# Two quarters of h gated in PSUM and copied out by ScalarE, and a longer queue before VectorE takes unhurried sums

## The chip, the cores and the metric

The program runs on one NeuronCore of a Trainium2 chip. The metric is the device time of one execution in microseconds, as the median of several runs. TensorE (PE) multiplies matrices into PSUM, eight banks of 512 fp32 columns. VectorE (DVE) and ScalarE (ACT) read and write PSUM and SBUF, GpSimd (POOL) works on SBUF alone, and SyncE (SP) issues the DMAs.

## The reference

Linear attention on 4 x 576 tokens feeds a mixture of eight experts, whose gate is normalised in eight Sinkhorn rounds, and then one wide feed-forward layer. What matters for the change is the expert layer and the last layer:

```python
for e in range(E):                      # E = 8; x is 2304 x 512, w1[e] 512 x 1024
    h = np.maximum(x @ w1[e], 0.0)
    out += P[:, e:e+1] * (h @ w2[e])    # w2[e] 1024 x 512
...
h = x @ w_in                            # 512 x 2048
g = h * (1.0 / (1.0 + np.exp(-1.702 * h)))
return g @ w_out                        # 2048 x 512
```

## The kernel before

Every matrix is split in two fp32r halves (a high part and the rest), and a product is three matmuls. Each 2 x 2 block product is done in seven products instead of eight, by sums of quarters of x, h and the weights. A *pair* is 512 columns of one expert's F (two halves c = 0 and 1 of 256 columns); a *visit* is one pair on one of three columns of 768 tokens. There are 16 pairs and 48 visits in layer 0 (the experts, `l` = 0) and 4 pairs and 12 visits in layer 1 (the last layer).

A visit makes h in `up_fast` (L1183), once for each half c, and multiplies it by w2 in `down_across` (L1346) in layer 0, `down` in layer 1. In `up_fast` the function `prod` multiplies one quarter of the weights into a bank (six matmuls on PE). The quarters of h are A11 (bank 2, called `pc`, the same bank for both halves), A22 (bank 7, `q`, the same for both), A12 (`ri`, bank 1 or 4) and a fourth that is never stored (`le`, bank 0 or 3). From them come S2, S1, N3 and S4, sums of quarters (`mixed`, L1221). `operand` (L1251) splits one of these seven into its high part `h..0` (an ACT copy) and the rest `h..1` (a subtraction). The subtraction is a DVE instruction if the source is a PSUM bank, and otherwise an SBUF sum of kind `VP`, which DVE or POOL may take. The tile names in rows and orders read h, half c, number of the operand (0 A11, 1 A12, 2 S2, 3 S1, 4 N3, 5 S4, 6 A22), part: `h161` is the rest of A22 of half 1. `gate` (L1233) applies ReLU and the token's gate P, of which a broadcast lies in `x2s`; layer 0 gates h itself from expert 1 on, and expert 0 is gated later in `acc`.

In layer 0 from expert 1 on, A11 and A22 are gated by DVE from their bank into the `ring` (SBUF buffers of 128 x 384), and their high part and rest are then made from the ring. A12 and the fourth quarter are gated in their banks. In layer 1, A11 and A22 stay in their banks, `operand` copies them to h and (argument `kept`) to the ring with two ACT copies, and DVE subtracts from the bank.

`down_across` goes through 14 turns of six matmuls (`TURNS`, L1329): A11 of both halves, S1 of half 0, A12 of both, S2 of both, S1 of half 1, then N3, S4 and A22 of both. After A11, ACT copies banks 5 and 6 into banks 0 and 1 (L1369), on which A12 goes on adding; S1 starts in banks 7 and 2; and from S2 on each group's end is added to `acc` by DVE (L1375) before the group's banks are used again.

The order of each engine's instructions comes from a planner (`Plan`, L27 on): it walks a list of all operations with their costs and due times and hands each engine the most urgent one that is ready. `VP` operations wait in one heap for DVE and POOL. DVE leaves the most urgent of them to POOL when its due time is more than `BELOW` = 2.5 us away and fewer than six are waiting (L152). PE's own order is fixed by the code. Beside all this, DVE and POOL turn the last layer's weights from fp64 words into fp32 (`double_piece`, L1113: six DVE operations of 128 x 512 on `x2s` at L1125 to L1141 and one POOL sum, 32 times, with due times from 440 to 1400 us), and POOL subtracts the high parts of all weights (`split`, L1094: `w1x` and `w2x`). Between the layers `y_operands` (L1024) makes layer 1's x from `acc` by more `VP` sums.

Of the kernel before, what the change touches and what calls it, by code (L numbers as in the profile page):

```python
# [24 lines left out]
class Plan:  # L25
# [86 lines left out]
    def run(self):  # L112
# [10 lines left out]
        m, done, t, bus, drift, out = 0, 0, 0.0, 0.0, 0.0, []  # L123
        self.stall = []
        while done < len(self.ops):
# [8 lines left out]
            for e in ("X", "PE", "DVE", "POOL", "ACT", "SP"):  # L134
# [12 lines left out]
                elif e in ("DVE", "POOL"):  # L147
                    own, both = sets[e], sets["VP"]
                    flex = both[0][2] if both else None
                    if flex is not None:  # L150
                        slack = flex.late - t + drift
                        if e == "DVE" and slack > self.BELOW and len(both) < 6:  # L152
                            flex = None
                        if e == "POOL" and slack < flex.dur["POOL"] - flex.dur["DVE"] and at["DVE"] < t + 0.5:
                            flex = None
# [45 lines left out]
def tile_performer_sinkhorn_moe(  # L201
# [981 lines left out]
    def up_fast(l, e, j, c):  # L1183
# [23 lines left out]
        def ring_of(i):  # L1207
            return (lambda: RT(i)), ("ring", i)

        def bank_of(b):  # L1210
            return (lambda: o(b)), ("b", b)
# [21 lines left out]
        def gate(b, th, out=None):  # L1233
            out = out or bank_of(b)
            rec(
                "DVE", ps_us(Q),
                lambda e: e.scalar_tensor_tensor(  # L1237
                    out=out[0](), in0=o(b), scalar=0.0, in1=T["G"][th], op0=ALU.max, op1=ALU.mult
                ),
                [("b", b), ("G", th)], [out[1]],  # L1240
            )
# [37 lines left out]
        for slot in (3, 2) if c == 0 else (2, 3):  # L1279
            yield  # L1280
            if slot == 3:
                prod(le, 3, 2, False)
                act(lambda: RT(u2), lambda: o(le), [("b", le)], [("ring", u2)])
                continue
            prod(pc, 2, 3, False)
            if done and not l:
                gate(pc, 0, ring_of(r11))
                operand(A11, ring_of(r11))
                continue
            swish(pc, 0)  # L1290
            operand(A11, bank_of(pc), True, r11)
        yield
        prod(le, 5, 4, False)
        dve(bank_of(q), bank_of(le), ring_of(r22), ALU.add)
        if done and not l:
            gate(q, 1, ring_of(r22))
            operand(A22, ring_of(r22))
        else:
            swish(q, 1)
            operand(A22, bank_of(q), True, r22)  # L1300
        tt(lambda: RT(s2), lambda: RT(r22), lambda: RT(r11), ALU.subtract, Q, [("ring", r22), ("ring", r11)], [("ring", s2)])
        yield
        prod(ri, 4, 5, False)
# [298 lines left out]
```

## Time and profile before

| | us |
|---|---|
| median of 3 runs | 1993.52 (1993.43 to 1993.97) |
| the profiled execution | 1992.32 |
| its span, first to last instruction | 1990.4 |
| PE busy | 1942.6 (98%) |
| DVE busy | 1483.2 (75%) |
| POOL busy | 1421.6 (71%) |
| ACT busy | 987.0 (50%) |

PE's busy time is modelled and hides short gaps. The weight loads (PEld) overlap the matmuls, and where PE runs without a gap they follow each other without one, so the time in which PEld stands still is the better measure of what PE loses. The granted TensorE clock is full in all stretches but around 1600 us and at the end.

### The profile page before, as it was taken

To read this page: it belongs to the slowest core of one execution; us is meant where nothing else is said; L and a number is where in the kernel's file an instruction comes from. 1 tells how busy PE (TensorE), PEld (TensorE's weight loads), DVE (VectorE), ACT (ScalarE), POOL (GpSimd) and SP (SyncE) were. 2 spreads that over 40 slices of the span, in tenths; PEclk is the share of its full clock that TensorE was granted. 3 is DMA by queue.
4 is the path that set the end of the run, shared out by engine and by line. 5 is a ranking of instruction groups with operands and counts; after the bars stand their busy time and mean duration, and the time that the engine had idled before them with its cause. 6 is when DMAs were issued, how large, how long until landed. Compare 5 with 4: busy or idle time off the path is not lost.

```text
span 1990.4 us, 36277 instructions
## 1 busy us (share of the span) xinstructions
PE 1942.6 (98%) x12899; PEld 1887.2 (95%) x12899; DVE 1483.2 (75%) x2762; ACT 987.0 (50%) x2225; POOL 1421.6 (71%) x1370
## 2 busy tenths in 40 slices
PE   8899999999999999999999999999999989999999
PEld 7788999999999999999999999999999989999999
DVE  7884467868788788878788887887866785656655
ACT  6884554444435344344434343443444566745654
POOL 5844375977869696878778696968787986838453
PEclk9999999999999999999999999999999999999999
DMA  9867456657658576676676585766765889645653
GB/s 171 218 169 241 175 201 243 229 206 283 225 222 293 198 268 242 223 273 241 229 268 234 214 300 200 258 256 218 253 246 201 290 308 321 252 165 224 233 199 130
DMA packets 259293, 464.06 MB, mean 233 GB/s; under 512 B 75288, under 2 KB 200104, under 8 KB 259112
## 3 DMA queue, kind: packets, MB, share of 16 engines
q1 hardware_dynamic: 259112, 461.74, 66.6%
q8 instruction: 102, 1.67, 0.3%
q14 instruction: 79, 0.65, 0.1%
HBM read 415.45 MB, written 46.21 MB: 232 GB/s over the span
## 4 chain that ended last, share of the span: by engine, by line
PE 78%; DVE 14%; ACT 3%; issue 2%; POOL 1%; DMA 1%; SPq 0%; DVEq 0%; ACTq 0%
PE bank L1195 35%; PE bank L1357 29%; PE bank L1394 8%; DVE h L429 4%; DVE ring L1216 2%; PE bank L598 2%; DVE bank L1216 1%; DVE bank L1237 1%; ACT acc L637 1%; DVE h L1216 1%; DVE ring L1237 1%; PE bank L576 1%; PE pair L704 1%; DVE x2s L1135 1%; PE bank L684 1%
## 5 line engine op out<-in xcount | busy, mean ns | idle before, releaser
L1195 PE MATMUL bank<-xo,w1x 128*128 128x384 f32 x5040 | 915.3, 336 | 3.7 <-ACT ring L1205 2.6
L1195 PEld LDWEIGHTS bank<-xo,w1x 128*128 128x128 f32 x5040 | 876.0, 188 | 9.9 <-DVE bank L1216 5.1
L1357 PE MATMUL bank<-h,w2x 128*128 128x384 f32 x4032 | 741.8, 338 | 19.5 <-DVE acc L1375 10.7
L1357 PEld LDWEIGHTS bank<-h,w2x 128*128 128x128 f32 x4032 | 698.5, 188 | 40.7 <-ACT bank L1369 15.6
L429 POOL TENSOR_TENSOR h<-ring,h 128x384 fp32r<-128x384 f32 x484 | 529.9, 1112 | 138.8 <-ACT h L1205 133.5
L1205 ACT ACTIVATE h<-ring 128x384 fp32r<-128x384 f32 x648 | 322.2, 526 | 241.6 <-DVE ring L1216 193.2
L1375 DVE TENSOR_TENSOR acc<-bank,acc 128x384 f32<-128x384 f32 x552 | 282.6, 550 | 136.8 <-PE bank L1357 130.9
L429 POOL TENSOR_TENSOR w1x<-raw,w1x 128x768 fp32r<-128x768 f32 (+1 forms) x120 | 184.3, 1545 | 221.6 <-ACT w1x L1101 221.4
L1205 ACT ACTIVATE bank<-bank 128x384 f32<-128x384 f32 x216 | 102.9, 479 | 399.6 <-PE bank L1195 390.7
L429 POOL TENSOR_TENSOR raw<-raw 128x256 f32<-128x256 f32 x309 | 231.0, 772 | 28.1 <-DMA raw<-in_moe_w_dram 14.2
L1205 ACT ACTIVATE ring<-bank 128x384 f32<-128x384 f32 x312 | 153.3, 492 | 161.1 <-PE bank L1195 151.2
L1216 DVE TENSOR_TENSOR ring<-bank,ring 128x384 f32<-128x384 f32 x432 | 225.2, 546 | 9.5 <-ACT bank L1205 6.1
L429 POOL TENSOR_TENSOR w2x<-raw,w2x 128x768 fp32r<-128x768 f32 (+1 forms) x120 | 190.9, 1598 | 15.5 <-ACT w2x L1101 15.3
L1394 PE MATMUL bank<-w2x,h 128*128 128x256 f32 x1512 | 186.7, 281 | 4.5 <-POOL w2x L429 2.2
L1394 PEld LDWEIGHTS bank<-w2x,h 128*128 128x128 f32 x1512 | 183.3, 189 | 6.9 <-DVE acc L1420 2.8
L429 POOL TENSOR_TENSOR ring<-ring 128x384 f32<-128x384 f32 x109 | 120.0, 1101 | 97.3 <-ACT ring L1205 48.7
L429 DVE TENSOR_TENSOR h<-ring,h 128x384 fp32r<-128x384 f32 x164 | 177.1, 1106 | 2.7 <-ACT h L1205 2.5
L1216 DVE TENSOR_TENSOR bank<-bank,ring 128x384 f32<-128x384 f32 x240 | 132.8, 558 | 41.4 <-PE bank L1195 39.8
L1237 DVE SCALAR_TENSOR_TENSOR ring<-bank,x2s 128x384 f32<-128x384 f32 x168 | 92.4, 550 | 75.7 <-PE bank L1195 75.2
L1216 DVE TENSOR_TENSOR h<-bank,h 128x384 fp32r<-128x384 f32 x156 | 85.9, 551 | 84.1 <-ACT ring L1205 61.1
L1237 DVE SCALAR_TENSOR_TENSOR bank<-bank,x2s 128x384 f32<-128x384 f32 x168 | 93.3, 555 | 22.3 <-PE bank L1195 21.9
L1101 ACT CAST w1x<-raw 128x768 fp32r<-128x768 f32 (+1 forms) x120 | 83.2, 697 | 45.2 <-PE bank L1195 43.3
(134 smaller groups left out, 1422.9 us busy)
## 6 DMA issues: line engine op xcount, KB each, us to landing
xo<-sx SPq DMA_DIRECT2D x413, 768.0 KB, 6.9
raw<-in_moe_w_dram SPq DMA_DIRECT2D x256, 128.0 KB, 3.4
x2s<-scr_g SPq DMA_DIRECT2D x90, 192.0 KB, 6.9
sx<-acc SPq DMA_DIRECT2D x46, 192.0 KB, 3.8
x2s<-in_moe_w_in_dram SPq DMA_DIRECT2D x16, 512.0 KB, 7.0
x2s<-in_moe_w_out_dram SPq DMA_DIRECT2D x16, 512.0 KB, 6.9
sx<-x2s SPq DMA_DIRECT2D x35, 192.0 KB, 4.0
sx<-xo SPq DMA_DIRECT2D x42, 128.0 KB, 3.2
```

The source lines that it names most:

```text
L429: lambda e: e.tensor_tensor(out=out(), in0=a(), in1=b(), op=op), r, w,
L576: nc.tensor.transpose(pt[:, i * P : (i + 1) * P], x[:, 2 * i : 2 * i + 2, :], ident)
L598: nc.tensor.matmul(pj[e][0][:, i * M : (i + 1) * M], xt[r, i * P : (i + 1) * P], om[r, :], start=True, stop=True, skip_group_check=True,)
L637: lambda h=h, pv=pv: nc.scalar.activation(f[:, h, :], pv[:, h // 2, :], AF.Exp, bias=nb[:, h : h + 1], scale=-1.0),
L1101: lambda e, a=a, b=b: nc.scalar.copy(T[w, c, 0][:, a:b], r[:, a:b]), raws, [(w, c, g, 0)],
L1195: nc.tensor.matmul(o(b), T["w1", c, a][:, slot, kk], T["xo"][x][:, y, kk], start=start and kk == 0 and n == 0, stop=kk == 1 and n == 2, sk ...
L1205: rec("ACT", act_us(Q), lambda e: nc.scalar.activation(out(), src(), f, **kw), r, w)
L1216: lambda e: e.tensor_tensor(out=out[0](), in0=a[0](), in1=b[0](), op=op), [a[1], b[1]], [out[1]],
L1237: lambda e: e.scalar_tensor_tensor(out=out[0](), in0=o(b), scalar=0.0, in1=T["G"][th], op0=ALU.max, op1=ALU.mult),
L1357: nc.tensor.matmul(bank[i][:, :Q], T["w2", c, y][:, slot, k * P : (k + 1) * P], T["h", c, a, x], start=s and m == 0, stop=c == 1 and m == ...
L1375: lambda e, i=i, q=q: e.tensor_tensor(out=q, in0=bank[i][:, :Q], in1=q, op=ALU.add), rd + [key], [key],
L1394: nc.tensor.matmul(bank[i][:, u], T["h", c, a, x][:, t * P : (t + 1) * P], T["w2", c, y][:, slot], start=s and m == 0, stop=c == 1 and m = ...
```

## The change

In layer 0 from expert 1 on, A11 and A22 are gated in their banks (`swish` calls `gate(b, th)`), as A12 is; ACT copies them from the bank to h and to the ring, and DVE subtracts from the bank. And DVE takes unhurried `VP` sums only from 14 waiting. Lines behind the change move up by eight: L1357, L1369 and L1375 become L1349, L1361 and L1367.

```diff
@@ Plan.run
-                        if e == "DVE" and slack > self.BELOW and len(both) < 6:
+                        if e == "DVE" and slack > self.BELOW and len(both) < 14:
                             flex = None
@@ up_fast
             prod(pc, 2, 3, False)
-            if done and not l:
-                gate(pc, 0, ring_of(r11))
-                operand(A11, ring_of(r11))
-                continue
             swish(pc, 0)
             operand(A11, bank_of(pc), True, r11)
         yield
         prod(le, 5, 4, False)
         dve(bank_of(q), bank_of(le), ring_of(r22), ALU.add)
-        if done and not l:
-            gate(q, 1, ring_of(r22))
-            operand(A22, ring_of(r22))
-        else:
-            swish(q, 1)
-            operand(A22, bank_of(q), True, r22)
+        swish(q, 1)
+        operand(A22, bank_of(q), True, r22)
```

In the built order PE's instructions stand as before, and all engines' orders are the same up to expert 1's first visit and again from the first visit of layer 1 on. In between, 168 gates of DVE write a bank instead of the ring; 168 `h` from ring subtractions are gone (153 from POOL, 15 from DVE) and 168 `h` from bank ones are new on DVE; ACT has 168 copies `ring<-bank` more; and 33 other `VP` sums have gone from DVE to POOL. In sum DVE has 120 instructions more, ACT 168 more and POOL 120 fewer.

DVE's order at the start of a visit on the first column (expert 4, at 990 us in the trace of before), from the first half's A11 gate on. Before:

```order
L1237 SCALAR_TENSOR_TENSOR ring_69<-bank2_101,x2s_75 128x384
L1129 SCALAR_TENSOR_TENSOR x2s_75<-x2s_75 128x512
L1216 TENSOR_TENSOR bank7_2526<-bank0_99,ring_69 128x384
L1132 TENSOR_SCALAR x2s_75<-x2s_75 128x512
L1237 SCALAR_TENSOR_TENSOR ring_69<-bank7_2526,x2s_75 128x384
L1216 TENSOR_TENSOR bank1_100<-bank1_100,ring_69 128x384
L1135 SCALAR_TENSOR_TENSOR x2s_75<-x2s_75 128x512
L1237 SCALAR_TENSOR_TENSOR ring_69<-bank2_101,x2s_75 128x384
```

The same place after:

```order
L1237 SCALAR_TENSOR_TENSOR bank2_101<-bank2_101,x2s_75 128x384
L1132 TENSOR_SCALAR x2s_75<-x2s_75 128x512
L1216 TENSOR_TENSOR h001_2369<-bank2_101,h000_2368 128x384
L1216 TENSOR_TENSOR bank7_2526<-bank0_99,ring_69 128x384
L1216 TENSOR_TENSOR bank1_100<-bank1_100,ring_69 128x384
L1237 SCALAR_TENSOR_TENSOR bank7_2526<-bank7_2526,x2s_75 128x384
L1237 SCALAR_TENSOR_TENSOR bank1_100<-bank1_100,x2s_75 128x384
L1135 SCALAR_TENSOR_TENSOR x2s_75<-x2s_75 128x512
L1216 TENSOR_TENSOR h061_2381<-bank7_2526,h060_2380 128x384
L1237 SCALAR_TENSOR_TENSOR bank2_101<-bank2_101,x2s_75 128x384
```

The gates write banks 2 and 7, and the rest of A11 (`h001`) stands on DVE behind a conversion step, ahead of the second use of bank 2.

DVE's order at the end of the same visit's rush, up to the first sum into `acc`. Before:

```order
L1141 SCALAR_TENSOR_TENSOR x2s_75<-x2s_75 128x512
L1216 TENSOR_TENSOR h111_2385<-bank4_103,h110_2384 128x384
L1216 TENSOR_TENSOR ring_69<-bank3_102,ring_69 128x384 x3
L429 TENSOR_TENSOR h121_2387<-ring_69,h120_2386 128x384
L429 TENSOR_TENSOR h131_2389<-ring_69,h130_2388 128x384
L429 TENSOR_TENSOR h141_2391<-ring_69,h140_2390 128x384
L1375 TENSOR_TENSOR acc0_72<-bank5_104,acc0_72 128x384
```

And after:

```order
L1141 SCALAR_TENSOR_TENSOR x2s_75<-x2s_75 128x512
L1216 TENSOR_TENSOR h111_2385<-bank4_103,h110_2384 128x384
L1216 TENSOR_TENSOR ring_69<-bank3_102,ring_69 128x384 x3
L429 TENSOR_TENSOR h121_2387<-ring_69,h120_2386 128x384
L429 TENSOR_TENSOR h141_2391<-ring_69,h140_2390 128x384
L1216 TENSOR_TENSOR ring_69<-bank4_103,ring_69 128x384
L1367 TENSOR_TENSOR acc0_72<-bank5_104,acc0_72 128x384
```

One of three SBUF subtractions (`h131`) has gone to POOL.

ACT's order around the copy of bank 3 into bank 2, with which the second half starts its A11. Before:

```order
L1205 ACTIVATE ring_69<-bank0_99 128x384
L1101 CAST w2x_71<-raw1_68 128x768
L1205 ACTIVATE bank2_101<-bank3_102 128x384
L1205 ACTIVATE h000_2368<-ring_69 128x384
L1101 CAST w2x_71<-raw1_68 128x512
```

And after:

```order
L1205 ACTIVATE ring_69<-bank0_99 128x384
L1205 ACTIVATE h000_2368<-bank2_101 128x384
L1205 ACTIVATE ring_69<-bank2_101 128x384
L1101 CAST w2x_71<-raw1_68 128x512
L1205 ACTIVATE bank2_101<-bank3_102 128x384
L1205 ACTIVATE ring_69<-bank4_103 128x384
```

The copy into bank 2 stands behind two reads of bank 2 and a cast, and it overwrites what DVE's `h001` reads.

## Rows read from the trace of the kernel before

**Rows 1.** Page, part 1: busy us, share of the span, instructions.

```profile
PE 1942.6 (98%) x12899; PEld 1887.2 (95%) x12899; DVE 1483.2 (75%) x2762; ACT 987.0 (50%) x2225; POOL 1421.6 (71%) x1370
```

**Rows 2.** Busy time by stretch: from expert 1 to the transition, and the transition.

```profile
core 0: us, PE busy (x) PEld busy (x) DVE busy (x) ACT busy (x) POOL busy (x), PEclk, DMA share, GB/s
346.00:1590.00 1244.00, 1225.02 (x6941) 1201.71 (x6941) 997.61 (x1738) 528.59 (x1080) 982.16 (x895) 1.00 0.68 243
1590.00:1680.00 90.00, 82.72 (x500) 79.27 (x500) 69.60 (x111) 63.72 (x147) 74.66 (x66) 0.96 0.92 320
```

**Rows 3.** Chain of waits (start us, us, what): same place, one and three visits apart.

```profile
428.87 12.49 PE bank L1357 x72
458.06 12.49 PE bank L1357 x72
...
836.90 12.48 PE bank L1195 x72
...
927.93 12.48 PE bank L1195 x72
```

**Rows 4.** Timeline 960 to 1019, PEld after a gap [idle before <- what ended it].

```profile
970.73 1.00 PEld L1195 LDWEIGHTS bank<-xo,w1x 128*128 128x128 f32 x6 [0.40 <-DVE bank L1216]
...
974.03 0.47 PEld L1357 LDWEIGHTS bank<-h,w2x 128*128 128x128 f32 x3 [0.19 <-ACT bank L1369]
...
974.82 9.85 PEld L1357 LDWEIGHTS bank<-h,w2x 128*128 128x128 f32 x57 [0.32 <-ACT bank L1369]
...
1004.75 0.82 PEld L1357 LDWEIGHTS bank<-h,w2x 128*128 128x128 f32 x5 [0.73 <-ACT bank L1369]
...
1006.17 3.80 PEld L1357 LDWEIGHTS bank<-h,w2x 128*128 128x128 f32 x22 [0.59 <-DVE h L1216]
...
1011.36 5.16 PEld L1357 LDWEIGHTS bank<-h,w2x 128*128 128x128 f32 x30 [1.39 <-DVE acc L1375]
```

**Rows 5.** The same timeline, DVE and one POOL row.

```profile
967.93 3.42 POOL L429 TENSOR_TENSOR w1x<-raw,w1x 128x768 fp32r<-128x768 f32 x2
968.03 2.17 DVE L429 TENSOR_TENSOR h<-ring,h 128x384 fp32r<-128x384 f32 x1
...
992.42 0.57 DVE L1216 TENSOR_TENSOR bank<-bank,ring 128x384 f32<-128x384 f32 x1 [0.74 <-PE bank L1195]
...
992.89 2.03 DVE L1132 TENSOR_SCALAR x2s<-x2s 128x512 uint32<-128x512 uint32 x1
...
1001.47 0.54 DVE L429 TENSOR_TENSOR h<-ring,h 128x384 fp32r<-128x384 f32 x1
...
1010.76 1.01 DVE L1375 TENSOR_TENSOR acc<-bank,acc 128x384 f32<-128x384 f32 x2
```

**Rows 6.** Chain of waits 1002 to 1012: DVE rows that follow each other without a gap.

```profile
1006.12 1.39 DVE ring L1216 x3
1007.51 3.33 DVE h L429 x3
```

**Rows 7.** Groups by line and shape: busy us, mean ns | idle before, releasers.

```profile
L429 POOL TENSOR_TENSOR h<-ring,h 128x384 fp32r<-128x384 f32 x484 | 529.9, 1112 | 138.8 <-ACT h L1205 133.5 <-DVE ring L1216 2.0 <-DMA raw<-in_moe_w_dram 1.2
...
L1205 ACT ACTIVATE ring<-bank 128x384 f32<-128x384 f32 x312 | 153.3, 492 | 161.1 <-PE bank L1195 151.2 <-POOL raw L429 5.1 <-POOL x2s L429 1.7
...
L1216 DVE TENSOR_TENSOR h<-bank,h 128x384 fp32r<-128x384 f32 x156 | 85.9, 551 | 84.1 <-ACT ring L1205 61.1 <-ACT h L1205 22.8
...
L1132 DVE TENSOR_SCALAR x2s<-x2s 128x512 uint32<-128x512 uint32 x32 | 32.9, 1027 | 0.0
```

**Rows 8.** Timeline 1690 to 1700 (layer 1): A11's high part on ACT, its rest on DVE.

```profile
1693.53 0.49 ACT L1205 ACTIVATE h<-bank 128x384 fp32r<-128x384 f32 x1
...
1694.44 0.56 DVE L1216 TENSOR_TENSOR h<-bank,h 128x384 fp32r<-128x384 f32 x1 [6.92 <-ACT ring L1205]
```

**Rows 9.** Timeline of PEld in the transition: two of its gaps.

```profile
1607.43 3.94 PEld L1357 LDWEIGHTS bank<-h,w2x 128*128 128x128 f32 x23 [0.81 <-ACT bank L1369]
...
1638.87 1.00 PEld L1394 LDWEIGHTS bank<-w2x,h 128*128 128x128 f32 x8 [2.51 <-POOL w2x L429]
```

## The prediction

> **What bounds the kernel now.** I read the page first: PE is busy 98% of the span [rows 1], so only PE's gaps can be won. They stand in the weight loads by stretch: from expert 1 to the transition (346 to 1590 us) PEld works 1201.7 of 1244 us, so 42.3 us are lost, and in the transition 10.7 of 90 [rows 2]. Outside these two stretches the change alters no order. Then the chain: a visit without a gap takes 458.06 - 428.87 = 29.2 us, but three visits at the 900th microsecond take 91.0 us instead of 87.6 [rows 3]. The timeline has the missing 3.6 us: 0.40 + 0.19 + 0.32 = 0.91 in the visit on the third column, 0.73 + 0.59 + 1.39 = 2.71 in that on the first, nothing on the second [rows 4]. Each ends with DVE or with ACT's copy into banks 0 and 1, which itself waits for DVE. The pattern repeats eleven times between 500 and 1440, the time of the weight conversion: 31 visits that lose 31 / 3 x 3.62 = 37.4 us; the other ten lose the remaining 4.9.
>
> So the place that matters is a rush on DVE in each visit: from the sum that starts the first half's A22 (PE has just ended that product) to the first sum into `acc`. PE has 16 products and turns of 12.49 / 12 = 1.04 us in between, 16.7 us. In the first column's visit DVE begins at 992.42 and ends the sum at 1011.3 [rows 5], 18.9 us, and PE came 2.71 late: 16.2 us are what DVE may take.
>
> **The prices.** DVE's instructions on a bank follow each other every 1.39 / 3 = 0.465 us, its SBUF sums beside a busy POOL every 3.33 / 3 = 1.1 us [rows 6]; a conversion step takes 1.03 [rows 7], 1.05 with its start. In the order of before the rush holds 21 bank instructions, 4 steps and 4 sums on the first column (9.8 + 4.2 + 4.4 = 18.4 us; one step took 2.03 us [rows 5], which makes up the 18.9 with little idle time), 22, 1 and 3 on the third (14.6), 22, 0 and 2 on the second (12.4).
>
> **What the change does, part by part.**
>
> A11 and A22, 168 each way. A gate costs DVE the same in a bank as into the ring. The rest of A11 or A22 was an SBUF sum (1.11 us, 153 of 168 on POOL [rows 7]); now it is a bank subtraction on DVE, 0.465 in the rush. DVE thus gets 168 x 0.55 = 92 us [rows 7] more, four instructions or 1.9 us in each of 42 visits.
>
> ACT gets 168 x 0.49 = 83 us [rows 7] more in 1244, where it is busy for 529 [rows 2]. I cost these at nothing by themselves: ACT's slack hides them. What they do to the bank is the slower rival below.
>
> The threshold. DVE loses 48 SBUF sums (15 of A11 and A22, 33 others), 48 x 1.1 = 53 us, and the rush loses most: on the first column 2 remain of 4. POOL has 120 fewer in all, 120 x 1.11 = 133 us of its 982 [rows 2, 7].
>
> The new rush. After the change the orders go in a cycle of six visits. Bank instructions, steps and sums: 24, 2, 2 (15.5 us); 24, 3, 2 (16.5); 24, 2, 2 (15.5); 24, 2, 3 (16.6); 25, 3, 2 (17.0); 25, 1, 1 (13.8). Over six visits that is 94.9 us; before it was 2 x 45.4 = 90.8. **The rush grows on average, but it is levelled**: no visit has 18.4 any more. Against 16.2 the lateness at the last deadline is 0, 0.3, 0, 0.4, 0.8 and 0: 1.5 us in six visits, the lower bound.
>
> Earlier deadlines bind sooner. I walk through the heaviest visit, the one in the second order fence, from the end of the first half's A22 product, with each DVE instruction not before its input: the gate of bank 0 starts at 6.1, the second half's A22 sum ends at 7.5 (PE wants bank 3 at 8.3), its rest `h161` at 10.0 (PE wants bank 7 for S1 at 10.4), the last read of bank 1 at 11.4, `h111` at 13.35 and `h121` at 15.8. Turn (1,1) wants `h111` at 12.5: about 1.0 late with the signal. The second turn of S2 then wants `h121` at 15.6: 0.4 more, 1.4 in all. In the two visits with 16.5 and 16.6 the last read of bank 1 ends at 12.1 and ACT's copy at 12.7, 0.8 after PE wants it, and `h121` adds 0.3: 1.2 and 1.1. The two with 15.5 lose 0.1 to 0.2, the last nothing. Sum: 4.0 us in six visits.
>
> The same walk over the old orders gives 0, 2.1 and 0 where the trace has 0.91, 2.71 and 0. What is missing, 1.55 in three visits, is single long instructions: an SBUF sum of 2.17 us that ran beside two weight subtractions of POOL, and the 2.03 us step, where the same sum takes 0.54 with POOL idle [rows 5]. The new rush has 13 steps and 12 sums in six visits (10 and 18 before), and POOL is busy for less; I add half as much, 1.6 in six visits. So 5.6 instead of 2 x 3.62 = 7.24. By bounds: 1.5 to 7.1 (the walk with the old extra), each way for 31 / 6 visits.
>
> Sum for the stretch: 37.4 us become 31 / 6 x 5.6 = 28.9. Of the ten visits without conversion two drop from 2.3 to 0.4 in the walk, so I take 3.0 for their 4.9. Together 42.3 becomes 31.9: **10.4 us gained**.
>
> The transition. From the first sum of `y_operands` to the second 768-wide subtraction of `w2x` POOL's order has 69 instructions before and 72 after, by the same prices 78.9 and 81.9 us. PE's longest gap there ends with just that subtraction [rows 9], so up to 3 us are lost; but the last visit of layer 0 gets rid of half its SBUF sums in the rush (17.5 us becomes 14.9), for which PE paid five gaps, 2.8 us in sum, the longest 0.81 [rows 9]. I take a net loss of 1.3, between -2.8 and +3.
>
> Profiled execution: 1992.3 - 10.4 + 1.3 = 1983.2; the median of the runs lies 1.2 above the profiled one, so **1984.4 us**.
>
> **A rule that speaks against it.** In layer 1, where A11 already goes this way, the high part starts on ACT at 1693.53 and DVE's subtraction at 1694.44, after both ACT copies of 0.49, and 61.1 us of DVE's idle time before such subtractions end with the ring copy [rows 7, 8]. The Trainium skill, PSUM — Partial Sum Buffer, section on bank collisions, says that ACT and DVE must not touch one bank at once, reads included. The trace agrees in that the two never overlap; if they could, the rest would be ready 0.4 us sooner, which would change no deadline above but bank 7's.
>
> **The rivals.**
>
> A, slower: bank 2 is held too long. The second half starts its A11 in bank 2, by ACT's copy from bank 3. That copy used to follow the gate; now it follows two ACT reads, a cast and DVE's `h001`, which stands behind a conversion step. PE wants the copy's end 2.1 us after the first half's A22 product; by the walk `h001` ends at 0.1 and the copy at 0.7. It decides at `h001` ending after 1.4. One step of 2.03 [rows 5] brings it to 1.1, a late cast in front of the copy beyond. If 35 of the visits lose 0.5 us, 17.5 us are lost: 1984.4 + 17.5 = 2001.9. For it: two engines in series now stand in front of a product of PE, where before one did. Against it: ACT is idle half of the time, and layer 1 does the same with little lost.
>
> B, the gain is larger. Where POOL rests, an SBUF sum of DVE takes 0.54 us instead of 1.1 [rows 5, 6]. If POOL's 133 us less work spares DVE the long cases and shortens the others, the rush falls to the walk's 4.0 or below, towards 1.5: 1984.4 - 31 / 6 x 1.6 = 1976 to 1984.4 - 31 / 6 x 4.1 = 1963, say 1973. [...]
>
> C, no difference: the new rush is longer on average, and if the long cases hit it as hard as the old one (7.1 in six visits), 37.4 becomes only 36.7; with 1.9 from the other visits 2.6 us are won, and the transition takes up to 3 back: 1991 to 1994.
>
> **How the numbers follow.** This kernel's measurement can tell about 0.2%, 4 us, from no change. My forecast (1979 to 1989.5) gets 0.47, B below 1979 0.18, C within 4 us of 1993.5 0.20, A 0.15. So faster 0.65, same 0.20, slower 0.15. The range leaves out B's last part and most of A: 1971 to 1996.
>
> **What would show it.** After the change PEld's gaps from 346 to 1590 should fall from 42 to about 32 us, spread over four or five visits of six with none above 2 us, and end with ACT L1361 (the copy into banks 0 and 1), DVE `h` L1216 and little with `acc` L1367. DVE's busy time rises by about 40 us, ACT's by 80, POOL's falls by 130. Gaps of PE in front of L1195 that end with ACT's `bank` L1205 would show rival A; gaps that end with POOL `h` would show a sum moved to POOL that comes too late, which I don't count. Conversion steps and sums on DVE well below 1.0 us on the mean would show B. A loss in the transition above 3 us makes the prediction wrong from there.

## The result and the profile after

The changed kernel takes 1968.38 us (median; 1967.68 to 1969.80), the kernel before beside it 1993.64 us (1993.43 to 1993.97): a ratio of 0.9874, 95% interval 0.9857 to 0.9891, or 25.3 us less. The prediction was 1984.4 with a range of 1971 to 1996: the sign was right, the size was missed by 16 us, and the time lies below the range. The profiled execution took 1969.8 us, its span is 1968.0, 22.4 us shorter than before.

First the page, then busy time by stretch (columns as in [rows 2]); 500 to 1440 us is the time of the weight conversion.

```profile
PE 1931.8 (98%) x12899; PEld 1888.0 (96%) x12899; DVE 1483.1 (75%) x2882; ACT 1044.7 (53%) x2393; POOL 1265.6 (64%) x1250
```

```profile
346.00:1590.00 1244.00, 1236.38 (x7054) 1223.12 (x7054) 1018.05 (x1893) 604.08 (x1285) 844.49 (x792) 1.00 0.70 248
500.00:1440.00 940.00, 933.05 (x5322) 922.82 (x5321) 786.66 (x1460) 452.88 (x962) 625.86 (x578) 1.00 0.70 249
1590.00:1680.00 90.00, 84.14 (x550) 82.02 (x549) 57.51 (x96) 59.81 (x142) 65.91 (x58) 0.98 0.87 310
```

From 346 to 1590 us PE's weight loads now stand idle for 1244.0 - 1223.1 = 20.9 us; before it was 42.3 [rows 2]. That is 21.4 of the 22.4 us. (The window is fixed in us. Followed instruction by instruction, the same work takes 20.2 us less, and the transition behind it 3.5 us less.) The most telling number is in the page: DVE has 120 instructions more than before and is busy for the same time, 1483.1 against 1483.2 us [rows 1]. The added bank instructions were paid for by 48 on-chip sums that DVE no longer makes, and by shorter sums and steps. The groups by line and shape show the shortening (mean ns behind the bar; before: DVE's `h<-ring` sums 1106, step L1132 1027 and POOL's `h` 1112 [rows 7]):

```profile
L1216 DVE TENSOR_TENSOR h<-bank,h 128x384 fp32r<-128x384 f32 x324 | 178.5, 551 | 114.4 <-ACT ring L1205 90.4 <-ACT h L1205 21.5
L429 DVE TENSOR_TENSOR h<-ring,h 128x384 fp32r<-128x384 f32 x130 | 121.5, 948 | 4.0 <-ACT h L1205 1.9
...
L1129 DVE SCALAR_TENSOR_TENSOR x2s<-x2s 128x512 uint32<-128x512 uint32 x32 | 40.2, 1257 | 0.5
...
L1125 DVE TENSOR_SCALAR x2s<-x2s 128x512 uint32<-128x512 uint32 x32 | 25.6, 801 | 0.1
L1135 DVE SCALAR_TENSOR_TENSOR x2s<-x2s 128x512 f32<-128x512 uint32 x32 | 24.9, 777 | 0.1
L1138 DVE TENSOR_SCALAR x2s<-x2s 128x512 uint32<-128x512 uint32 x32 | 20.4, 638 | 0.0
...
L1132 DVE TENSOR_SCALAR x2s<-x2s 128x512 uint32<-128x512 uint32 x32 | 17.6, 551 | 0.0
```

Not all steps got shorter: L1129 rose from 903 to 1257 ns and L1125 from 506 to 801, the other four fell, and the six together take 159.9 us instead of 175.0.

What PE's weight loads waited for from 346 to 1590 us (us in total, times, longest), before and then after:

```profile
PEld bank L1357 <- DVE acc L1375: 15.1, 14, 1.4
PEld bank L1357 <- ACT bank L1369: 14.2, 35, 0.7
PEld bank L1357 <- DVE h L1216: 6.5, 12, 0.6
PEld bank L1195 <- DVE bank L1216: 4.4, 11, 0.4
```

```profile
PEld bank L1349 <- ACT bank L1361: 6.7, 12, 0.8
PEld bank L1349 <- DVE acc L1367: 4.6, 10, 0.7
PEld bank L1349 <- DVE h L1216: 4.3, 8, 0.6
PEld bank L1195 <- ACT bank L1205: 2.3, 5, 0.5
PEld bank L1349 <- POOL h L429: 1.4, 3, 0.5
```

The same producers end the gaps, for far less time; `ACT bank L1205` is new and is the mechanism of the slower rival, 2.3 us in five places. One cycle of six visits now loses 3.05 us, in three of the six visits (before: 7.24). Its gaps on the timeline are

```profile
607.61 3.95 PEld L1349 LDWEIGHTS bank<-h,w2x 128*128 128x128 f32 x23 [0.50 <-ACT bank L1361]
612.03 5.86 PEld L1349 LDWEIGHTS bank<-h,w2x 128*128 128x128 f32 x34 [0.47 <-POOL h L429]
627.74 5.16 PEld L1195 LDWEIGHTS bank<-xo,w1x 128*128 128x128 f32 x30 [0.45 <-ACT bank L1205]
639.05 3.79 PEld L1349 LDWEIGHTS bank<-h,w2x 128*128 128x128 f32 x22 [0.58 <-DVE h L1216]
643.35 5.17 PEld L1349 LDWEIGHTS bank<-h,w2x 128*128 128x128 f32 x30 [0.52 <-DVE acc L1367]
...
726.78 9.85 PEld L1349 LDWEIGHTS bank<-h,w2x 128*128 128x128 f32 x57 [0.53 <-ACT bank L1361]
```

### The profile page after: what moved, and what is told of

Same layout as the page of the kernel before. It is cut to its first block, busy times and chain, and to the rows that moved or that the text cites. A ratio compares the mean times of both kernels' runs of the same rounds, so it can differ in the third digit from the quotient of the medians.

```text
span 1968.0 us, 36376 instructions
## 1 busy us (share of the span) xinstructions
PE 1931.8 (98%) x12899; PEld 1888.0 (96%) x12899; DVE 1483.1 (75%) x2882; ACT 1044.7 (53%) x2393; POOL 1265.6 (64%) x1250
## 4 chain that ended last, share of the span: by engine, by line
PE 78%; DVE 12%; ACT 3%; issue 3%; POOL 2%; DMA 1%; SPq 0%; DVEq 0%; ACTq 0%; POOLq 0%
PE bank L1195 35%; PE bank L1349 29%; PE bank L1386 8%; DVE ring L1216 2%; DVE bank L1237 2%; DVE h L1216 2%; PE bank L598 2%; DVE h L429 2%; DVE bank L1216 1%; ACT acc L637 1%; PE bank L576 1%; POOL h L429 1%; PE pair L704 1%; PE bank L684 1%; PE pair L654 1%
## 5 line engine op out<-in xcount | busy, mean ns | idle before, releaser
L1349 PE MATMUL bank<-h,w2x 128*128 128x384 f32 x4032 | 734.4, 337 | 7.4 <-ACT bank L1361 3.0
L1349 PEld LDWEIGHTS bank<-h,w2x 128*128 128x128 f32 x4032 | 700.1, 188 | 19.5 <-ACT bank L1361 6.7
L429 POOL TENSOR_TENSOR h<-ring,h 128x384 fp32r<-128x384 f32 x350 | 375.1, 1087 | 152.4 <-ACT h L1205 130.3
L1367 DVE TENSOR_TENSOR acc<-bank,acc 128x384 f32<-128x384 f32 x552 | 282.5, 551 | 141.7 <-PE bank L1349 135.1
L1205 ACT ACTIVATE h<-ring 128x384 fp32r<-128x384 f32 x480 | 239.2, 529 | 152.7 <-DVE ring L1216 143.7
L1205 ACT ACTIVATE ring<-bank 128x384 f32<-128x384 f32 x480 | 235.4, 492 | 148.2 <-PE bank L1195 143.3
L1205 ACT ACTIVATE bank<-bank 128x384 f32<-128x384 f32 x216 | 103.1, 480 | 386.1 <-PE bank L1195 347.9
L1216 DVE TENSOR_TENSOR h<-bank,h 128x384 fp32r<-128x384 f32 x324 | 178.5, 551 | 114.4 <-ACT ring L1205 90.4
L1237 DVE SCALAR_TENSOR_TENSOR bank<-bank,x2s 128x384 f32<-128x384 f32 x336 | 183.9, 558 | 67.6 <-PE bank L1195 66.7
L1205 ACT ACTIVATE h<-bank 128x384 fp32r<-128x384 f32 x360 | 176.3, 492 | 53.2 <-DVE bank L1237 38.4
L429 POOL TENSOR_TENSOR w2x<-raw,w2x 128x768 fp32r<-128x768 f32 (+1 forms) x120 | 182.8, 1535 | 23.8 <-ACT w2x L1101 23.3
L429 DVE TENSOR_TENSOR h<-ring,h 128x384 fp32r<-128x384 f32 x130 | 121.5, 948 | 4.0 <-ACT h L1205 1.9
L1101 ACT CAST w2x<-raw 128x768 fp32r<-128x768 f32 (+1 forms) x120 | 81.5, 694 | 56.3 <-POOL raw L429 51.4
```

Of the source, the lines that this page charges most:

```text
L429: lambda e: e.tensor_tensor(out=out(), in0=a(), in1=b(), op=op), r, w,
L1101: lambda e, a=a, b=b: nc.scalar.copy(T[w, c, 0][:, a:b], r[:, a:b]), raws, [(w, c, g, 0)],
L1205: rec("ACT", act_us(Q), lambda e: nc.scalar.activation(out(), src(), f, **kw), r, w)
L1216: lambda e: e.tensor_tensor(out=out[0](), in0=a[0](), in1=b[0](), op=op), [a[1], b[1]], [out[1]],
L1237: lambda e: e.scalar_tensor_tensor(out=out[0](), in0=o(b), scalar=0.0, in1=T["G"][th], op0=ALU.max, op1=ALU.mult),
L1349: nc.tensor.matmul(bank[i][:, :Q], T["w2", c, y][:, slot, k * P : (k + 1) * P], T["h", c, a, x], start=s and m == 0, stop=c == 1 and m == ...
```

## The experiments

Every time below stands beside runs of the kernel before on the same chip (their median 1993.1 to 1995.0 us), and "gaps" is PEld's idle time from 346 to 1590 us: 42.3 before, 20.9 after.

### Gating and threshold apart

The changed kernel with the old threshold, and the old gating with the new threshold:

```diff
-if e == "DVE" and slack > self.BELOW and len(both) < 14:
+if e == "DVE" and slack > self.BELOW and len(both) < 6:
```

> The gating and the rests of A11 and A22 as in the changed kernel, the threshold left at 6. The order of VectorE in every conversion visit is then that of the changed kernel; only at the transition of 1586 to 1660 us do seven on-chip sums stand on another engine. Theory 1 (the gain is made in the conversion visits, by VectorE's rush losing its sums and meeting fewer GpSimd reads): 1967 to 1972 us, and weight-load gaps of 346 to 1590 us at 21 us as in the changed kernel. Rival (the threshold keeps sums out of the rush, and that is the gain): 1980 to 1990 us, gaps above 32 us.

> The kernel before with the threshold at 14 and nothing else. VectorE's order changes by about eleven sums, all at the transition. Theory 1: 1990 to 1994 us, gaps of 346 to 1590 us still 42 us. Rival (the threshold is the gain): 1968 to 1982 us.

Gating alone: 1974.1 us (ratio 0.9906, 0.9891 to 0.9920), gaps 23.6. Threshold alone: 1996.1 us (1.0016, 1.0006 to 1.0025), gaps 44.8. So the gating is the gain, in the visits, and the threshold does two different things. On the old gating it costs 3 us: from 1590 to 1680 us POOL is busy for 77.2 us instead of 74.7, and PE waits for it twice more:

```profile
PEld bank L1394 <- POOL w2x L429: 3.1, 1, 3.1
...
PEld bank L1357 <- POOL h L429: 2.4, 2, 1.2
```

On the new gating, which leaves POOL room (65.9 us there), the same sums moved to POOL give 5.7 us (the intervals of the two ratios just touch); 3.0 of them are gaps of PEld from 1555 to 1600 us, 4.3 us at threshold 6 and 1.3 at 14. Theory 1 had the direction, but both kernels came out above its ranges (1967 to 1972 and 1990 to 1994 us); that the threshold would add so much, or lose by itself, it had not said.

### Who has to be relieved: VectorE or GpSimd

Three kernels with the old orders. The A11 and A22 rests are cut to 8 columns where POOL makes them (152 in the stretch), or where DVE makes them (15), or on POOL with two fills behind each, which read nothing and write a tile that has no reader before the transition, so that POOL stays as long in its queue:

```diff
+def rest(e):
+    n = 8 if a in (A11, A22) and e is nc.gpsimd else Q     # second kernel: nc.vector
+    e.tensor_tensor(out=g()[:, 0:n], in0=src[0]()[:, 0:n], in1=h()[:, 0:n].bitcast(F32), op=ALU.subtract)
+    for _ in range(2 if n < Q else 0):                     # third kernel alone
+        e.memset(SIG, 0.0)
-tt(g, src[0], lambda: h().bitcast(F32), ALU.subtract, Q, [src[1], hk], [gk])
+rec("VP", both_us(Q), rest, [src[1], hk], [gk])
```

> The kernel before, same order on every engine; the A11 and A22 rests of the first layer from the second expert on that GpSimd makes are cut from 384 columns to 8 (the rest of them is left out), those that VectorE makes stay whole. Theory 1 (VectorE's steps and sums are long because GpSimd reads beside them): conversion steps L1132 to L1138 fall from 1.0 to 0.55 to 0.8 us, gaps of 346 to 1590 us from 42 to 25 to 32 us, 1975 to 1985 us. Theory 2 (VectorE's own queue, fewer on-chip sums of its own in the rush): gaps 38 to 43 us, 1988 to 1994 us.

> The kernel before, same order; now those of the same rests that VectorE makes are cut to 8 columns and GpSimd's stay whole. Theory 1: the conversion steps stay at 1.0 us, gaps 33 to 40 us, 1984 to 1991 us. Theory 2: gaps 42 to about 22 us, 1968 to 1976 us. Both may hold in part; then this gain and that of the cut on GpSimd add up to about the 25 us of the change.

> As the cut on GpSimd, but two fills of an unused 128x384 tile (0.43 us each) behind each cut rest, so that GpSimd's queue is as long as before and reads less. If reads are what meets VectorE: steps and gaps as with the cut alone, within 3 us of it. If GpSimd's own time in its queue (or any use of its port, writes too) is what counts: as the kernel before, 1990 to 1995 us.

POOL relieved: 1969.1 us (0.9872, 0.9857 to 0.9887), gaps 19.1. DVE relieved: 1988.6 (0.9970, 0.9958 to 0.9981), gaps 37.5. POOL as long in its queue but reading less: 1985.6 (0.9954, 0.9937 to 0.9971), gaps 33.3, between its two expectations. **The whole 25 us can be had without touching DVE's order at all**, by taking work off POOL (here most of each rest is left out). Theory 2 falls. Theory 1 had the direction, but more came than it said, and not by its mark: in the first kernel the steps stayed at 0.82 to 1.0 us on the mean, and it was the sums that shrank (1114 to 874 ns).

What POOL does to DVE is seen at one sum, the same in three kernels (timeline, POOL and DVE). Before:

```profile
818.23 1.30 POOL L429 TENSOR_TENSOR w2x<-raw,w2x 128x512 fp32r<-128x512 f32 x1
...
818.32 1.62 DVE L429 TENSOR_TENSOR h<-ring,h 128x384 fp32r<-128x384 f32 x1
```

With POOL's rests cut:

```profile
810.09 1.30 POOL L429 TENSOR_TENSOR w2x<-raw,w2x 128x512 fp32r<-128x512 f32 x1
...
812.08 0.54 DVE L1264 TENSOR_TENSOR h<-ring,h 128x384 fp32r<-128x384 f32 x1
812.23 1.27 POOL L429 TENSOR_TENSOR ring<-ring 128x384 f32<-128x384 f32 x1 [0.85 <-DVE ring L1237]
```

With the fills:

```profile
815.95 1.29 POOL L429 TENSOR_TENSOR w2x<-raw,w2x 128x512 fp32r<-128x512 f32 x1
816.01 1.65 DVE L1265 TENSOR_TENSOR h<-ring,h 128x384 fp32r<-128x384 f32 x1
...
823.07 1.49 DVE L1265 TENSOR_TENSOR h<-ring,h 128x384 fp32r<-128x384 f32 x3
823.62 0.89 POOL L1267 MEMSET sig<- 128x384 f32 x2
```

With its rests cut POOL was ahead of its work and rested 0.85 us when DVE's sum came; the sum took 0.54. Before and with the fills it was in a weight rest, and the sum was held for a microsecond. At 823.07 three sums beside a fill take 0.5 each; before, the three in the same place took 3.41. So the 25 us have two parts: about 9 us because POOL no longer reads in the cut rest's place, and about 16 because a POOL that is ahead is elsewhere in its queue when DVE comes. The parts are nearer to equal than these times say: one gap of 3.45 us of the kernel with fills stands at 1562 us behind a DMA of the transition, and from 346 to 1540 us the gaps are 42.3 us before, 29.8 with the fills and 17.3 with the rests cut. The second part shows at the sum that took 2.17 us before [rows 5]. With the fills, and then with the rests cut:

```profile
963.18 2.19 DVE L1265 TENSOR_TENSOR h<-ring,h 128x384 fp32r<-128x384 f32 x1
```

```profile
957.75 1.18 DVE L1264 TENSOR_TENSOR h<-ring,h 128x384 fp32r<-128x384 f32 x1
```

The three gaps behind it (0.91 us before [rows 4], 0.94 with the fills) are gone only with the rests cut. Only one gap of the kernel with fills, 0.5 us, ends with POOL itself; it is not POOL's results that were late.

How often DVE meets POOL can be counted from the start and end times in the traces (346 to 1590 us; spans on POOL are rough). In the kernel before, all 126 `h<-ring` sums of DVE begin while POOL is in an operation, and each lasts as long as that operation still has to go plus 0.4 to 0.5 us, at least 0.54. In the changed kernel 17 of 96 begin beside a resting POOL, and these take 0.54 or 0.55.

The kernel with DVE's rests cut adds a sharp row. A sum of 8 columns has next to nothing to do, and its mean is 1463 ns:

```profile
L1264 DVE TENSOR_TENSOR h<-ring,h 128x8 fp32r<-128x8 f32 x15 | 22.0, 1463 | 0.6 <-ACT h L1205 0.6
```

### Half of it

POOL's rests of A11 or of A22 alone cut, in the old orders; and the changed kernel with only one of the two quarters gated in its bank.

```diff
-n = 8 if a in (A11, A22) and e is nc.gpsimd else Q
+n = 8 if a == A11 and e is nc.gpsimd else Q    # the other kernel: a == A22
```

> The kernel before, same order; only the A11 rests that GpSimd makes are cut to 8 columns (the rest of them is left out), A22's stay whole. Both cut gave 1969.1 us. If the relief of GpSimd adds up: 1980 to 1984 us, gaps about 32 us. If most of it hangs on one quarter: near 1970 us here or with A22 and near 1990 us with the other. If a hold is only avoided when GpSimd has rested through: both 1986 to 1994 us.

> As the last, with A22's rests cut instead of A11's. Additive: 1980 to 1984 us. A22's rests stand at the head of the rush and of GpSimd's queue there, so if one quarter carries it, this is the one: 1970 to 1978 us. Interaction: 1986 to 1994 us.

```diff
 prod(pc, 2, 3, False)
+if done and not l:
+    gate(pc, 0, ring_of(r11))
+    operand(A11, ring_of(r11))
+    continue
```

This is A22 alone; for A11 alone the old lines come back behind the sum into bank `q` in the same way.

> The changed kernel with A11 gated out of its bank as before; A22 alone gated in its bank and copied out. The rush of a conversion visit begins with A22's sum, so if the gain is made in the rush, most of it is here: 1970 to 1978 us. If it is made by freeing GpSimd and VectorE anywhere, about half: 1978 to 1984 us. If both quarters are needed for it, above 1986 us.

> The changed kernel with A22 gated out of its bank as before; A11 alone gated in its bank and copied out. A22 alone gave 1996.3 us, since one VectorE sum in the first visit's rush there took 1.80 us beside a GpSimd weight rest and PE then waited 1.02 us. Theory 1 (a sum or step is short if GpSimd rests when it starts, long if GpSimd is in an operation; each new order decides that anew): A11 alone lies anywhere between 1972 and 1996 us, and the us lost in its visits follow the number of h sums and steps over 1.2 us between A22's sum and the first acc sum. Rival (each quarter is worth its half of the relieved work, and A22's half was spoilt by something of its own): 1980 to 1984 us.

Cut on POOL: A11 1986.5 us (0.9959, 0.9944 to 0.9974), A22 1982.4 (0.9932, 0.9916 to 0.9949). In an unchanged order the relief nearly adds up: 8.5 + 12.6 = 21.1 of 25.3. Gated alone: A22 1996.3 (1.0019, 1.0004 to 1.0033), A11 1999.9 (1.0030, 1.0018 to 1.0042), neither of them faster than before, and A11 above the 1996 us of theory 1. (The profiled execution of A22 alone took 2007.3 us, so its rows show the order rather than the median's loss.) There each change makes the planner write a new order, and the new order decides which sum meets a busy POOL. With A22 alone one does so in every third visit (91 us apart), early in the rush:

```profile
788.99 1.83 POOL L429 TENSOR_TENSOR w1x<-raw,w1x 128x768 fp32r<-128x768 f32 x1
...
789.43 1.80 DVE L429 TENSOR_TENSOR h<-ring,h 128x384 fp32r<-128x384 f32 x1
...
793.26 2.39 PEld L1353 LDWEIGHTS bank<-h,w2x 128*128 128x128 f32 x14 [1.02 <-DVE h L1216]
```

In the changed kernel the corresponding sum comes 0.01 us behind a POOL rest, goes first, and it is POOL's rest that lasts 1.72 instead of 1.3 us:

```profile
781.47 1.72 POOL L429 TENSOR_TENSOR w1x<-raw,w1x 128x512 fp32r<-128x512 f32 x1 [0.26 <-ACT w1x L1101]
781.48 0.55 DVE L429 TENSOR_TENSOR h<-ring,h 128x384 fp32r<-128x384 f32 x1
```

With A11 alone 33 gaps end with such a sum (10.7 us) and 34 with ACT's copy behind it (20.1 us). The rival's "half each" fell.

Visit by visit the us lost do follow the number of long sums and steps, as theory 1 says. Counted are the `h` sums and conversion steps over 1.2 us between A22's sum and the first `acc` sum, in the visits from 500 to 1440 us; the loss is the mean of PEld's gaps up to the next visit:

| kernel | long ones in a visit: us lost |
|---|---|
| before | 1: 0.00; 2: 0.92; 5: 2.74 |
| A11 alone | 2: 0.06; 3: 1.44; 4: 2.85 |
| A22 alone | 0: 0.00; 2: 1.06; 3: 2.48 |
| changed | 0: 0.20; 1: 0.39; 2: 1.17 |

### More work for GpSimd

Behind the 120 bank subtractions of experts 2 to 6, one POOL difference of an unused tile, or three fills of it:

```diff
 o.fn(ENGINES.get(e))
+if o.tag:
+    nc.gpsimd.tensor_tensor(out=SIG, in0=SIG, in1=SIG, op=ALU.subtract)   # or 3 x nc.gpsimd.memset(SIG, 0.0)
```

> The changed kernel, and behind each subtraction that now reads a bank (first layer, experts 2 to 6, A11 and A22: 120 places) one GpSimd difference of a 128x384 tile that nothing uses, about 1.0 us each: GpSimd reads on-chip memory there about as it did before the change, while VectorE's and ScalarE's queues stay as changed. Theory 1, ports (VectorE's on-chip sums and conversion steps got short because GpSimd reads less): conversion steps L1132, L1138, L1135 back from 0.55 to 0.78 us to about 1.0, VectorE h<-ring sums back from 0.9 to 1.1 us, gaps of 346 to 1590 us from 21 to about 30 us, time 1976 to 1982 us. Theory 2 (the new order of VectorE's queue alone): the same steps may be longer, but gaps 21 to 23 us and 1967 to 1971 us. Theory 3 (GpSimd's own queue was late): as theory 1 in time, but with gaps that end with a GpSimd h, and the next kernel loses as much.

> The changed kernel, and at the same 120 places three GpSimd fills of the unused 128x384 tile: GpSimd is as busy or busier, but reads nothing. Theory 1, ports: if only reads meet, conversion steps stay at 0.55 to 0.78 us, gaps at 21 to 24 us, 1967 to 1972 us. Theory 3 (GpSimd's own queue late): gaps ending with a GpSimd h, and as many us lost as with the differences, 1976 to 1982 us. Theory 2: 1967 to 1971 us.

2010.8 us (1.0100, 1.0071 to 1.0128) and 2042.5 us (1.0246, 1.0229 to 1.0263), with gaps of 59.7 and 88.5. This pair doesn't answer what it was made for. The planner does not know of the added 108 and 155 us, so POOL's own results come late: 21.9 and 47.9 us of the gaps end with POOL's `h`, theory 3, whether it reads or writes. The steps did not go back to 1.0. One thing fits the holds: the kernel with reads has a DVE sum of 5.57 us.

### What ends a hold

POOL's weight rests of 512 or 768 columns made in pieces of 256, on the kernel before and on the changed one; then short fills as pauses, on the changed kernel and on that with pieces:

```diff
-tt(T[w, c, 1][:, a:b], r[:, a:b], T[w, c, 0][:, a:b], ALU.subtract, (b - a) * FC, ..., eng="POOL")
+for i in range(a, b):                          # one POOL entry of the plan, two or three operations
+    e.tensor_tensor(out=T[w, c, 1][:, i : i + 1], in0=r[:, i : i + 1], in1=T[w, c, 0][:, i : i + 1].bitcast(F32), op=ALU.subtract)
```

```diff
 o.fn(ENGINES.get(e))
+if e == "POOL" and tags[0] <= o.n <= tags[-1]:
+    nc.gpsimd.memset(SIG[:, 0:8], 0.0)
```

> The kernel before, same order; GpSimd's weight rests (384 of 512 or 768 columns: 1.3 to 1.95 us each) are made as two or three operations of 256 columns, about 0.75 us each. GpSimd is some 40 to 60 us busier in all. Theory 1a (a VectorE operation that finds GpSimd in an operation waits for the end of that one operation): VectorE h<-ring sums from 1.11 to about 0.95 us, conversion steps from 1.0 to 0.75 to 0.9 us, gaps of 346 to 1590 us from 42 to 30 to 37 us, 1982 to 1990 us. Theory 1b (the two share the port column by column, or GpSimd's whole busy time counts): sums and steps as long as before, gaps 42 to 48 us, 1994 to 2002 us.

> The changed kernel with the same weight rests in pieces of 256 columns. Theory 1a: the remaining 21 us of gaps fall to 15 to 20 us, 1962 to 1968 us. Theory 1b, or GpSimd's queue as the tighter thing: 1970 to 1978 us.

> The changed kernel with a fill of 8 columns of an unused tile behind each GpSimd operation of the first layer's experts 2 to 6 (about 420). Theory 1c (a VectorE operation with two on-chip inputs that comes while GpSimd is in a sum is let in only when GpSimd's reading pauses; a fill reads nothing and is a pause): VectorE h<-ring sums from 0.92 to at most 0.75 us, gaps of 346 to 1590 us from 21 to 13 to 20 us, 1962 to 1970 us, GpSimd's added time against it. Theory 1d (a fill is no pause; only an empty GpSimd queue is): sums as long as in the changed kernel and GpSimd later, 1970 to 1980 us.

> The kernel with the weight rests in pieces on the changed kernel (2000.2 us, one VectorE sum of 17.75 us beside 17 GpSimd sums in a row, five others of about 5 us beside GpSimd's pieces) with the same fills of 8 columns from experts 2 to 6, behind the pieces of a rest but not between them. Theory 1c: the sums of about 5 us fall below 2.5 us; the one of 17.75 us, which lies ahead of expert 2's fills if it lies in expert 1, stays where no fills are. Gaps ending with a VectorE h<-ring, 11.75 us in 500 to 1440 us, fall below 3 us. Theory 1d: the sums of about 5 us stay.

Pieces on before: 1994.9 us (1.0009, 0.9997 to 1.0021), gaps 41.6: five of the six steps fell (now 0.54 to 0.99 on the mean), the sums stayed at 1.09, and from 500 to 1440 us 31 gaps, 9.3 us in sum, now end with a later POOL `h`. Pieces on the changed kernel: 2000.2 us (1.0046, 1.0015 to 1.0076), spread from 1988 to 2016, where neither theory had put it. Theory 1a, that a held operation waits for the end of one POOL operation, fails at this row (profiled run of 2015.6 us, POOL, DVE and PEld):

```profile
373.15 18.22 DVE L429 TENSOR_TENSOR h<-ring,h 128x384 fp32r<-128x384 f32 x2
373.55 1.03 POOL L429 TENSOR_TENSOR acc<-acc,x2s 128x384 f32<-128x384 f32 x1
374.53 1.01 POOL L429 TENSOR_TENSOR h<-ring,h 128x384 fp32r<-128x384 f32 x1
375.49 13.36 POOL L429 TENSOR_TENSOR acc<-acc,x2s 128x384 f32<-128x384 f32 x14
388.81 0.73 POOL L429 TENSOR_TENSOR raw<-raw 128x256 f32<-128x256 f32 x1
389.49 1.00 POOL L429 TENSOR_TENSOR acc<-acc,x2s 128x384 f32<-128x384 f32 x1
390.95 2.10 PEld L1351 LDWEIGHTS bank<-h,w2x 128*128 128x128 f32 x7 [16.44 <-DVE h L429]
```

One DVE sum was held for 17.75 us while POOL ran 18 sums on end, and PE lost 16.4 us by it. In the changed kernel, at the same place, DVE got in sooner (2.72 us for the two sums). So a hold can end between two POOL operations, and need not. Theory 1a is the rule all the same: it describes all 126 sums of the kernel before, as counted above, and all 129 of the kernel with POOL's rests cut; of the kernels with pieces, 14 sums of 126 (before) and 5 of 90 (changed) were held for longer than the one operation. With fills the longest such sum of the stretch is 1.45 us (17.75 without them) and the gaps that end with one fall from 32.0 to 0.3 us; the time is 1989.1 (0.9993, 0.9963 to 1.0023), lost again to gaps of 10.5 us that end with the fills behind POOL's late `h`. That is what theory 1c expects of the sums of about 5 us. It does not prove it: the 17.75 us sum lies ahead of the first fill and went too, so its absence there is not the fills' doing, and the profiled runs compared are the slowest of the ten without fills (2015.6 us) and the fastest of the ten with them (1979.1). Fills on the changed kernel: 1973.9 (0.9898, 0.9883 to 0.9912), sums 0.96 us instead of 0.92, gaps 25.7: what theory 1d expects, with nothing to gain where holds are short, and 52 us more for POOL. What decides whether a waiting DVE operation is let in between two POOL operations stays open.

### The planner's numbers

The threshold at 20 (the same order up to 60), and the other bound at 0:

```diff
-BELOW = 2.5
+BELOW = 0.0
```

> The changed kernel with the threshold at 20 instead of 14; from 20 to 60 the order is the same, so the threshold then acts only through the due times. VectorE's order differs in about 75 places, at the first conversion visit of each stretch and the transition. If the threshold's gain (5.7 us between 6 and 14, on the changed gating) goes on: 1962 to 1967 us. If it only happened to place seven sums of the last conversion visit well: 1967 to 1972 us.

> The changed kernel with the planner's other bound at 0 instead of 2.5 us: VectorE takes an unhurried on-chip sum (below 14 waiting) only when its due time is past; VectorE's order changes in some 65 places, mostly ahead of 400 us and at the transition. If fewer sums on VectorE mean fewer holds: 1962 to 1968 us. If GpSimd is then later with them: 1969 to 1976 us.

Threshold 20: 1967.6 us (0.9871, 0.9855 to 0.9887), not to be told from 14. Bound 0: 1992.7 (0.9995, 0.9979 to 1.0011), far above both expectations: the gain is gone. DVE has 35 `h<-ring` sums in the stretch instead of 96, but those 35 last 1294 ns on the mean, up to 4.76 us: fewer of them, and each held longer beside a POOL that is 30 us busier:

```profile
PEld bank L1349 <- DVE h L429: 15.0, 23, 4.0
PEld bank L1195 <- ACT ring L1205: 8.2, 10, 0.9
```

No version beat the changed kernel by more than the measurement can tell.

## Why the prediction was right or wrong

**The bound and the place: right.** The gain came from PEld's gaps between 346 and 1590 us (21.4 of 22.4 by the window, 20.2 by instruction), ended by the producers that were named.

**Walking the orders: right in form, a little dear.** The walk gave 4.0 us in six visits, the trace has 3.05. For the heaviest visit it said 1.4, and the trace of 975 to 1003 us has 0.45 + 0.60 + 0.50 = 1.55:

```profile
984.22 5.15 PEld L1195 LDWEIGHTS bank<-xo,w1x 128*128 128x128 f32 x30 [0.45 <-ACT bank L1205]
...
995.55 3.78 PEld L1349 LDWEIGHTS bank<-h,w2x 128*128 128x128 f32 x22 [0.60 <-DVE h L1216]
...
999.83 3.26 PEld L1349 LDWEIGHTS bank<-h,w2x 128*128 128x128 f32 x19 [0.50 <-DVE acc L1367]
```

**The step that failed: the 1.6 us for single long instructions.** I saw that the old walk missed 1.55 us in three visits, named the cause (a 2.17 us sum, a 2.03 us step beside POOL [rows 5]) and carried half of it over because the new rush holds about as many sums and steps. None came: no gap of the cycle is above 0.58. 31 / 6 x 1.6 = 8.3 us of the miss. The prices of 1.05 and 1.1 are the same mistake in the small: they are means over holds that the change takes away in part. Steps L1132 and L1138 fell to 0.55 and 0.64 (all six from 0.91 to 0.83), the sums from 1.11 to 0.92 in the stretch. If the walk's whole difference to 3.05 is put down to that, it is another 31 / 6 x 0.95 = 4.9 us. The two make 13.2; from 500 to 1440 us as a whole the miss is 28.9 - 17.2 = 11.7, since other cycles lose a little more than this one.

**"POOL has 120 fewer" was the gain, and was costed at nothing.** The forecast took POOL's 133 us off its queue and gave no price to it outside rival B. The kernel with POOL's rests cut shows that relief of POOL alone (882 us busy from 346 to 1590 us, 982 before) is worth 25 us with DVE's order as it was. One row was misread on the way: the sum of 0.54 us at 1001.47 [rows 5] was not short beside an idle POOL. POOL was in this subtraction and had 0.12 us to go:

```profile
1000.29 1.30 POOL L429 TENSOR_TENSOR w2x<-raw,w2x 128x512 fp32r<-128x512 f32 x1
```

So what a sum costs was set by how much of POOL's operation was left when it came, which a mean does not carry over to another order.

**The other visits: too much by 1.5 us.** I took 4.9 to 3.0; followed by instruction, the work outside 500 to 1440 us lost 3.5 us before and loses 3.1 now.

**The transition: wrong in sign.** A loss of 1.3 was forecast; the gaps of 0.3 us and more there were 9.6 us in sum and are 7.2, by the timelines. POOL's second `w2x` is late as forecast, by little (its gap is 2.61 us where it was 2.51 [rows 9]), and a gap of 2.40 that ends with ACT's cast into `w2x` is new, but the rush ahead of it, which cost 2.8 us in five gaps, costs 0.8 now, and a gap of 2.20 behind ACT's ring copy is down to 0.69. The threshold makes part of this, and only together with the gating.

**The median: 2.6 us.** The forecast put the median 1.2 us above the profiled execution; it came 1.4 us below.

**Busy times.** DVE +40 forecast, -0.1 measured; ACT +80, +57.7; POOL -130, -156. The first is the price error again: 168 bank instructions cost 92.6 us as forecast, the 48 sums that left DVE gave back what the forecast had counted, and shorter sums (1.06 to 0.95 us on the mean of all) and steps gave back the rest.

**The bank rule: no deadline moved, as forecast.** DVE's idle time behind ACT's ring copy rose from 61.1 [rows 7] to 90.4 us (first group above), and the gaps that end with a bank subtraction into `h` fell from 6.5 to 4.3 us.

**The rivals.** B was the case that came, with its mechanism: the forecast put it at 1973 and gave it 0.18. The rows that should have weighed more were in hand: 0.54 against 2.17 [rows 5] is a factor of four on the very instructions that were late, and the change took 11% of POOL's work. A's wait exists (2.3 us in five places, 0.5 at most) and is more than seven times smaller than its price. C fell with the long cases.

## What to carry to other kernels

When a sum with both inputs on chip leaves GpSimd or VectorE, price the meetings that it takes away, not only the instruction: VectorE's bank subtractions into `h` took 539 to 559 ns each whatever GpSimd did, its on-chip sums 541 to 2172. Don't price the new order with means of the old one when the change relieves the engine that made them long; take the undisturbed duration as one bound and the old mean as the other. And after a change of a planner's rule look at which operations now start together: neither half of this change gained anything, and the same relief in an unchanged order nearly added up.

## What the runs showed of the hardware

A VectorE sum of two on-chip inputs that comes while GpSimd is in such an operation is held. Mostly it lasts what is left of that operation plus 0.4 to 0.5 us (all 126 of the kernel before); a few were held for two operations (1.46 us), for four to six (about 5 us) or, once, for 19 (17.75 us for 0.54 us of work). A small width does not help (8 columns: 1.46 us). It also goes the other way: GpSimd's rest took 1.72 instead of 1.3 us where VectorE went first. There the two began 0.01 us apart; at 959.46 us of the changed kernel they began 0.02 us apart and VectorE was held (1.69 us), so who goes first at such a distance is not shown. Fills on GpSimd did not hold the three sums beside them (0.50 each).

Conversion steps with a single on-chip input (L1125, L1132, L1138) are held too: in the kernel before 35 of 96 began beside a resting GpSimd and took 0.41 to 0.43 us, the others up to 2.03.

VectorE's instructions with one input in a bank are not touched: the 1403 of the kernel before from 346 to 1590 us took 0.54 to 0.57 us, of which 1157 began while GpSimd was in an operation. The 252 bank subtractions into `h` from 346 to 1590 us of the changed kernel lie within 20 ns (min/median/max ns); the on-chip sums into `h` of the kernel before in the same stretch are spread fourfold:

```profile
L1216 DVE TENSOR_TENSOR h<-bank,h x252: 539/548/559, 359.2 to 1586.6; 128x384 fp32r<-128x384 f32 x126
```

```profile
L429 DVE TENSOR_TENSOR h<-ring,h x126: 541/1130/2172, 359.9 to 1578.6; 128x384 fp32r<-128x384 f32 x126
```

The Trainium skill, SBUF — State Buffer, section "Who interferes with whom", says that a VectorE instruction with two SBUF inputs contends with GpSimd operations that read and not with those that only write, and that the order of issue decides who waits. The rows agree with the first part; who waits they do not decide for starts 0.02 us apart. That a hold can go on through many GpSimd operations it does not say.
